# Overlapping feature tiles, B turned straight from DRAM, and the fourth state input of two chunks in one unit

## The chip, the core and the metric

The kernel runs on one core of a Trainium2 chip. The metric is the device time in microseconds. A core has five engines that run beside each other: TensorE (PE, matrix products into PSUM, which has eight banks), VectorE (DVE), ScalarE (ACT), GpSimd (POOL) and SyncE (SP, which issues the DMAs here). Each engine takes its instructions in the order in which they were written; semaphores tie the engines together.

## The reference

The input x has 2048 tokens of 448 features. It is normalised per token, and two branches read the result xn:

```python
xn = _layernorm(x)
# branch A: a diagonal complex recurrence over the tokens, 448 states
Lam_bar = exp(dt * (Lambda_re + 1j * Lambda_im));  B_bar = ((Lam_bar - 1) / Lam) * (B_re + 1j * B_im)
h_t = Lam_bar * h_{t-1} + B_bar @ xn_t
s = 2 * real(C @ h) + xn * Dskip
# branch B: a gated network with 1792 hidden features
g = silu((sigmoid(xn @ w_gate) * (xn @ w_up)) @ w_down)
out = x + s * g
```

## The kernel before

**Chunks and tiles.** The tokens go in four chunks of 512 (c = 0 to 3), each of four tiles of 128. The 448 features are the contracted dimension of most products. They are kept, turned, in `xnT[c]` as four tiles of 128 rows: features 0 to 127, 128 to 255, 256 to 383, and a fourth tile that holds features 384 to 447 twice, once in each half of 64 rows. The second copy is made by `ln_turn` (L272, chunk 0) and `ln_twice` (L277, the others) before the turning; PE turns chunk 0 (L274), DMA transposes on SP turn the others (L270). The weights of gate and up have the first 384 rows in `wg` and `wu`, and the last 64 rows of both stand under each other in `wt`: gate in the upper half of the rows, up in the lower half. So gate takes its tail from one copy of the features and up from the other.

**Halves.** From the fifth group of hidden features on, PE works with two halves of 64 rows that run beside each other. A sum (`Sum`, L504) has seven products of 64 rows, because 448 is seven times 64; some of them run in the upper half and some in the lower one. Where a sum changes halves, its next product waits for the last one of the other half by way of an empty instruction (a "word") in POOL's queue (L512). A unit is either one group of 128 hidden features (`gu_unit`, two sums, gate and up) or one state input (`bu_unit`). States 0 to 383 are three state inputs of two sums, real and imaginary. The fourth state input holds the last 64 states, real in one half of the output's partitions and imaginary in the other; it is one sum with four products in the upper half and three in the lower.

**Pairs of units.** `duo` (L1050) runs two units: first the upper half of the first unit beside the lower half of the second, then the other way round. Behind the second step ScalarE empties the four PSUM banks (the `empty` functions: sigmoid and a copy for a group of hidden features, L740; copies for a state input, L570 and L631), and what else stands in `beside` for that place is emitted (`rest`). `fill` then emits VectorE's pieces of the recurrence (phase factors, the scan along the tokens, phase factors again) as far as PE's time of that step allows; it takes them from the two oldest units that have any left. A line of each chunk gives the order of pairs (L1080 to L1083): negative numbers are state inputs, -4 being the fourth. `emit_downs` (the product with w_down of the chunk before) and `emit_ys` (the product with C) stand between them. In the fourth state input the halves of the partitions have to be swapped before VectorE can combine real and imaginary; two DMAs do this (`swap_halves`, L529), for the input and again after the scan.

**B and C.** B's real and imaginary rows are loaded into `raw_re` and `raw_im` as they are, the last 64 columns are doubled (L153, L288, L289), and eight DMA transposes (`emit_b`, L297) make `bT`, the stationary operand of the state inputs. C's rows are loaded in the second half of chunk 0 into `raw_c` and `raw_re` and turned by eight DMA transposes (L169) at the first two groups of chunk 1: first the four of `tc_re`, then the four of `tc_im`. `emit_c` (L457) mixes them into `ct`; each of its seven mixes is a scaled copy on ScalarE into a scratch (L482) and a product and sum on VectorE (L483). The first three ScalarE parts stand at `"down1"` of chunk 1, ahead of the reading of that chunk's down sums (sigd L764, zb L766). A list `c_room` (L467) says where the scratches lie: the first two in the room of `raw_im`, two in the pool's own, two in the room of `raw_c`, one in the pool's own. A room is written again only when all that read its earlier contents has ended.

**Order.** `keep_order` fixes the written order on each engine. SP's queue has, in order: x of chunk 0, the weights' columns 0 to 511, B, the weights' columns 512 to 1023, x of chunk 1, then the first B transpose, the weights' columns 1024 to 1791 with another B transpose between them, skip, four B transposes, x of chunk 2, two transposes of chunk 1's xn, the last two B transposes, two more of xn, w_down, C, and then the swaps and the C transposes.

Of the kernel before, what the change touches and what calls it, by code (L numbers as in the profile page):

```python
# [10 lines left out]
FP32 = mybir.dt.float32  # L11
# [18 lines left out]
NPK = 2 * D  # L30
EPS = 1e-5
# [7 lines left out]
def swap_pair(ap: bass.AP) -> bass.AP:  # L39
    step_p, n_p = ap.ap[0]  # L40
    step_m, n_m = ap.ap[1]
    step_f, n_f = ap.ap[2]
    assert n_m == 2
    return bass.AP(tensor=ap.tensor, offset=ap.offset + step_m,
                   ap=[[step_p, n_p], [-step_m, n_m], [step_f, n_f]])

# [17 lines left out]
def kernel(  # L64
# [51 lines left out]
    def load_rows(eng, t, mat, f0, f1):  # L116
        eng.dma_start(out=t[:, 0:3, f0:f1], in_=mat[0:384, f0:f1].rearrange("(kt p) f -> p kt f", p=P))
        eng.dma_start(out=t[0:64, 3, f0:f1], in_=mat[384:448, f0:f1])

    def load_w(eng, f0, f1, between=None):  # L120
        for t, mat in ((wg, B_w_gate), (wu, B_w_up)):
            eng.dma_start(out=t[:, :, f0:f1], in_=mat[0:384, f0:f1].rearrange("(kt p) f -> p kt f", p=P))
        if between:
            between()
        for mat, p0 in ((B_w_gate, 0), (B_w_up, 64)):
            eng.dma_start(out=wt[p0:p0 + 64, f0:f1], in_=mat[384:448, f0:f1])
# [130 lines left out]
    def ln_norm(c, j):  # L257
        t = c * TPC + j
        xb = xn[c % 3]
        if c < 2:  # L260
            dve.tensor_scalar(out=xb[:, j, 0:D], in0=x_t[c][:, j, :], scalar1=mv[:, t, 0:1],
                              scalar2=rsd[:, t, :], op0=ALU.subtract, op1=ALU.mult)
        else:
            act.activation(xb[:, j, 0:D], x_t[c][:, j, :], ACT.Identity, bias=nmr[:, t, :],
                           scale=rsd[:, t, :])

    def ln_turn(c, j):
# [4 lines left out]
        (dve if j < 2 else pool).tensor_copy(out=xb[:, j, D:DP], in_=xb[:, j, 384:D])  # L272
# [3 lines left out]
    def ln_twice(c, copy, j0=0, j1=TPC):  # L276
        copy(out=xn[c % 3][:, j0:j1, D:DP], in_=xn[c % 3][:, j0:j1, 384:D])  # L277
        for j in range(j0, j1):
            ln_turn(c, j)
# [6 lines left out]
    def emit_b_twice():  # L286
        t = raw["b_im"]
        act.copy(out=t[:, 0:3, D:DP], in_=t[:, 0:3, 384:D])  # L288
        act.copy(out=t[0:64, 3, D:DP], in_=t[0:64, 3, 384:D])  # L289

    def emit_b(cc, pt):
        n = P if pt < 3 else 64
        if cc == 0:
            p0 = pt * P
        else:
            p0 = D if pt == 3 else 512 + pt * P
        sync.dma_start_transpose(out=bT[:, :, p0:p0 + n], in_=raw[("b_re", "b_im")[cc]][0:n, pt, :])  # L297

    def bu_cols(pt, cc):
        if pt == 3:  # L300
            return 384, 512
        return (pt * P, (pt + 1) * P) if cc == 0 else (512 + pt * P, 512 + (pt + 1) * P)
# [104 lines left out]
    def emit_skip(c):  # L407

        t = xn[c % 3][:, :, 0:D]
        dve.tensor_tensor(out=t, in0=t, in1=bcast_mid(skip[:], TPC), op=ALU.mult)  # L410
# [46 lines left out]
    def emit_c(i):  # L457
# [9 lines left out]
        if not c_room:  # L467
            for nm in ("raw_im", "raw_c"):
                both = []
                c_room.extend((nm, both, k) for k in range(2))  # L470
                if nm == "raw_im":
# [57 lines left out]
    def swap_halves(o, i):  # L529
        sync.dma_start(out=o[0:64, :], in_=i[64:128, :])  # L530
        sync.dma_start(out=o[64:128, :], in_=i[0:64, :])

    def bu_unit(c, pt):
        u = Unit()
        psts = [bank("bu") for _ in range(2 if pt < 3 else 1)]
        sums = [Sum(t, 7) for t in psts]

        def ops(h, cc, n):
            lo, hi = bu_cols(pt, cc)
            return [(sums[cc], (bT[HALF[h], kt, lo:hi], xnT[c][HALF[h], kt, :], 0, TC))  # L540
                    for kt in range(n)]

        if pt < 3:
            u.top = ops(0, 0, 4) + ops(0, 1, 3)
            u.bot = ops(1, 0, 3) + ops(1, 1, 4)
        else:
            u.top, u.bot = ops(0, 0, 4), ops(1, 0, 3)
        u.empty, u.then = bu_after(c, pt, psts)
        return u

    def bu_after(c, pt, pst):
# [5 lines left out]

        def then():
            unread[0] += 1
            assert unread[0] <= 4  # L560
            stream[0] += 1
            popped[stream[0]] = clock[0]
            pieces.extend((*p, stream[0]) for p in line)
# [62 lines left out]
        else:  # L626
            bus = sp.tile([P, TC], BF16, name="bus3", tag="bus", bufs=4)
            bsw = sp.tile([P, TC], BF16, name="bsw3", bufs=1)

            def empty_3():  # L630
                act.copy(out=bus[:], in_=pst[0][:])  # L631
                swap_halves(bsw, bus)

            empty = [empty_3]

            def q0():
                T["ta"] = sp.tile([P, TC], BF16, name="ta3", tag="ta")
                dve.tensor_tensor(out=T["ta"][:], in0=bus[:], in1=cosT[:, 3, :], op=mul)
# [511 lines left out]
```

## Time and profile before

| what | value |
|---|---|
| runs of the kernel, device time | 184.78, 184.30, 184.43 us; median 184.43 |
| profiled execution, its span from first to last instruction | 182.6 us |
| PE busy | 177.7 us, 1644 products |
| VectorE busy | 165.0 us |
| ScalarE busy | 114.1 us |
| POOL busy | 24.5 us |
| DMA queue of SP, share of the 16 engines' span | 35.1%, 14.79 MB |
| granted TensorE clock | 1.000 |

The profile gives the span of its own execution and no other time for it; the runs' median lies 1.83 us above that span, for what lies before the first and after the last instruction. A line of the timeline has the start in us, the duration in us, the engine, the line of the program, the operation, what it writes and reads, and in brackets the idle time of the engine before it with what ended that. "SPq" is SP's queue: the duration there is that of issuing the DMA, not of the transfer. Products are pipelined: a product of 512 columns is shown with 0.38 us while another one starts every 0.216 us in the same half.

### The profile page before, as it was taken

What the parts mean: (1) busy time and instruction counts of PE and PEld (TensorE: products, weight loads), DVE (VectorE), ACT (ScalarE), POOL (GpSimd) and SP (SyncE); (2) the same over time, 40 slices, a digit from 0 to 9 for tenths busy, and PEclk for the clock granted to TensorE, in tenths of its full rate; (3) what the DMA queues carried; (4) which work ended last, traced back from release to release, by engine and by line L of the source; (5) the groups of instructions that cost most, each with busy time, mean ns of one, the idle gap of its engine ahead of it and who ended that gap; (6) DMA issues with size and microseconds to landing.
All of it is one profiled execution on the core that took longest, in us unless ns stands there. A gap on an engine that the chain in (4) does not pass through costs nothing.

```text
span 182.6 us, 4348 instructions
## 1 busy us (share of the span) xinstructions
PE 177.7 (97%) x1644; PEld 98.3 (54%) x1644; DVE 165.0 (90%) x337; ACT 114.1 (63%) x236; POOL 24.5 (13%) x61
## 2 busy tenths in 40 slices
PE   7999999999999999999999999999999999999992
PEld 7776644446654444645654445545665544645552
DVE  4899999799989979999999999599999999699983
ACT  3999577979487787997367766057048567144100
POOL 4768546321000000004000000000000000000000
PEclk9999999999999999999999999999999999999999
DMA  5999997895434113011251010030001000011112
GB/s 152 312 307 252 231 161 106 229 311 111 104 76 89 29 32 101 4 52 52 41 79 29 4 29 0 4 101 0 4 2 29 4 13 17 4 50 50 29 36 68
DMA packets 27659, 15.07 MB, mean 83 GB/s; under 512 B 16243, under 2 KB 27638, under 8 KB 27638
## 3 DMA queue, kind: packets, MB, share of 16 engines
q1 hardware_dynamic: 27632, 14.79, 35.1%
q8 instruction: 13, 0.21, 0.5%
q14 instruction: 8, 0.07, 0.2%
q10 hardware_dynamic: 6, 0.00, 0.0%
HBM read 8.49 MB, written 1.84 MB: 57 GB/s over the span
## 4 chain that ended last, share of the span: by engine, by line
PE 97%; DVE 1%; POOL 0%; issue 0%; POOLq 0%; DVEq 0%
PE g_ps L510 25%; PE u_ps L510 19%; PE d_ps L510 17%; PE bu L510 12%; PE y_ps L510 11%; PE d_ps L1093 6%; PE warm_ps L192 2%; PE g_ps L702 2%; PE u_ps L702 1%; PE tp_x L274 1%; PE g_ps L695 1%; DVE sg L846 0%; DVE o_l L852 0%; DVE xnT L282 0%; POOL ident L129 0%
## 5 line engine op out<-in xcount | busy, mean ns | idle before, releaser
L510 PE MATMUL u_ps<-xnT,wu 64*128 64x512 bf16 x312 | 68.9, 376 | 0.0
L510 PE MATMUL g_ps<-xnT,wg 64*128 64x512 bf16 x312 | 62.0, 376 | 0.0
L740 ACT ACTIVATE sig<-g_ps 128x512 bf16<-128x512 f32 x52 | 29.1, 597 | 29.1 <-PE g_ps L510 29.1
L510 PE MATMUL bu<-xnT,bT 64*128 64x512 bf16 x196 | 45.7, 376 | 0.0
L510 PEld LDWEIGHTS <-wu 64*128 64x128 bf16 x312 | 25.3, 94 | 17.8 <-POOLq L512 1.6
L510 PE MATMUL d_ps<-wd,hF 64*128 64x448 bf16 x336 | 32.9, 349 | 0.0
L510 PEld LDWEIGHTS <-wg 64*128 64x128 bf16 x312 | 22.7, 94 | 17.6 <-POOLq L512 1.9
L740 ACT CAST ub<-u_ps 128x512 bf16<-128x512 f32 x52 | 29.3, 604 | 0.8 <-DVE hF L712 0.8
L510 PEld LDWEIGHTS <-hF 64*128 64x128 bf16 x336 | 19.9, 94 | 12.1
L510 PEld LDWEIGHTS <-bT 64*128 64x128 bf16 x196 | 17.7, 94 | 10.7
L510 PE MATMUL y_ps<-ct,h 64*128 64x448 bf16 (+2 forms) x203 | 22.7, 343 | 0.0
L589 DVE TENSOR_TENSOR_SCAN wv<-r_col,st,ta 128x512 bf16<-128x512 f32 x18 | 22.6, 1274 | 0.1
L737 DVE TENSOR_TENSOR hF<-sig,ub 128x512 bf16<-128x512 bf16 x52 | 20.9, 416 | 1.3 <-ACT ub L740 1.1
L510 PE MATMUL u_ps<-xnT,wt 64*128 64x512 bf16 x52 | 19.6, 376 | 0.0
L510 PE MATMUL g_ps<-xnT,wt 64*128 64x512 bf16 x52 | 19.6, 376 | 0.0
L510 PEld LDWEIGHTS <-h 64*128 64x128 bf16 (+1 forms) x203 | 13.4, 95 | 8.0
L570 ACT CAST bus<-bu 128x512 bf16<-128x512 f32 x24 | 14.3, 595 | 2.3 <-PE g_ps L510 2.3
L764 ACT ACTIVATE sigd<-d_ps 128x448 bf16<-128x448 f32 x12 | 6.6, 550 | 12.4 <-PE d_ps L510 12.4
L238 POOL TENSOR_TENSOR rsd<-ve,mhalf 128x1 f32<-128x1 f32 (+2 forms) x8 | 7.5, 932 | 48.5 <-PE u_ps L510 45.6
L510 PEld LDWEIGHTS <-wt 64*128 64x128 bf16 x104 | 9.8, 94 | 5.5 <-DMA wt<-in_B_w_up_dram 0.4
L1093 PE MATMUL d_ps<-wd,hF 128*128 128x448 bf16 x56 | 10.9, 353 | 0.0
L819 DVE TENSOR_TENSOR o_t<-y_ps,xn 128x448 bf16<-128x448 f32 x12 | 6.9, 618 | 3.7 <-PE y_ps L510 3.7
(153 smaller groups left out, 229.8 us busy)
## 6 DMA issues: line engine op xcount, KB each, us to landing
wd<-in_B_w_down_dram SPq DMA_DIRECT2D x1, 1568.0 KB, 7.6
x<-in_A_x_dram SPq DMA_DIRECT2D x3, 448.0 KB, 5.5
out_dram<-o_t SPq DMA_DIRECT2D x6, 224.0 KB, 2.1
wg<-in_B_w_gate_dram SPq DMA_DIRECT2D x2, 384.0 KB, 4.4
wu<-in_B_w_up_dram SPq DMA_DIRECT2D x2, 384.0 KB, 5.3
wg<-in_B_w_gate_dram SPq DMA_DIRECT2D x1, 576.0 KB
wu<-in_B_w_up_dram SPq DMA_DIRECT2D x1, 576.0 KB, 8.6
bsw<-bus SPq DMA_DIRECT2D x8, 64.0 KB, 2.0
```

The source lines that it names most:

```text
L192: pe.matmul(warm_ps[:], lhsT=ident[:], rhs=ident[:], start=True, stop=True)
L238: pool.tensor_tensor(out=rsd[:, t:t + n, :], in0=ve[:, t:t + n, :], in1=mhalf[:, 0:n, :], op=ALU.pow)
L274: pe.transpose(tps[j % 2][:, kt, :], xb[:, j, kt * P:(kt + 1) * P], ident[:])
L510: m = pe.matmul(self.t[:, n0:n1], lhsT=lhsT, rhs=rhs, start=self.done == 1, stop=self.done == self.n)
L570: empty = [lambda cc=cc: act.copy(out=bus[:, cc, :], in_=pst[cc][:]) for cc in range(2)]
L589: dve.tensor_tensor_scan(out=T["wv"][:, cc, :], data0=rb, data1=T["ta"][:, cc, :], initial=(0.0 if c == 0 else st[pt][:, cc, :]), op0=mul, ...
L702: pe.matmul(t[:, n0:n1], lhsT=wm[:, kt, f0:f1], rhs=xnT[c][:, kt, n0:n1], start=(first and kt == 0), stop=(not first and kt == 2))
L737: dve.tensor_tensor(out=h[:], in0=sig[:], in1=ub[:], op=ALU.mult)
L740: u.empty = [lambda: act.activation(sig[:], gt[:], ACT.Sigmoid), lambda: act.copy(out=ub[:], in_=ut[:])]
L764: act.activation(sigd[:], ds[j][:], ACT.Sigmoid)
L819: dve.tensor_tensor(out=o[:, i, :], in0=ys[c, j + 2 * i][:], in1=xb[:, i, :], op=ALU.add)
L1093: pe.matmul(ds[j][:], lhsT=hF[c, ft][:, j * P:(j + 1) * P], rhs=wd[:, ft, :], start=ft == 0, stop=ft == FT - 1)
```

## The change

Seven things change together.

1. The four turned feature tiles begin at features 0, 128, 192 and 320 (`K_ROWS`), so that they overlap: tile 1 holds 128 to 255, tile 2 holds 192 to 319. Gate takes tiles 0, 2 and 3 whole and features 128 to 191 from the upper half of tile 1; up takes tiles 0, 1 and 3 whole and features 256 to 319 from the lower half of tile 2. The doubling copies (L272, L277) are no longer there. For chunks 1 to 3 the norm writes 512 columns, as two runs of 256 that overlap in the source; what reads xn later (skip, the last sums) reads two runs of 224.
2. B isn't loaded into SBUF. Four DMA transposes read it in DRAM, each 448 rows and 256 columns. The copies that doubled its last columns are gone. The columns of the fourth state input are gathered into `b3` by two POOL copies at group 9 of chunk 0.
3. `load_w` has six DMAs for a range of columns, not four, since the rows of gate and up are cut differently; the second range is 512 to 1279 and the third 1280 to 1791.
4. The fourth state input of chunks 0 and 1 is one unit with two sums, at its place in chunk 0, and that of chunks 2 and 3 one unit at its place in chunk 2. It has two banks, two ScalarE copies, one swap of twice the size, and one list of VectorE's pieces for both chunks.
5. In chunks 1 and 3 there is then no fourth state input; `duo` becomes `group`, which also takes three units, and (5,6), (-4,7) becomes (5,6,7) there.
6. With `raw_im` gone, the first two scratches of the mixing lie in the room of `raw_re`, and the scratches of the last chunk's rest in `raw_re` and `raw_c`.
7. The B transposes stand together on SP ahead of the weights' last columns.

```diff
+K_ROWS = (0, 128, 192, 320)
+GATE_K, UP_K = (0, 2, 3), (0, 1, 3)
...
+        eng.dma_start(out=wg[:, 1:3, f0:f1], in_=rows(B_w_gate, 192, 448))
+        eng.dma_start(out=wg[:, 0, f0:f1], in_=rows(B_w_gate, 0, 128))
+        eng.dma_start(out=wu[:, 0:2, f0:f1], in_=rows(B_w_up, 0, 256))
+        eng.dma_start(out=wu[:, 2, f0:f1], in_=rows(B_w_up, 320, 448))
+        eng.dma_start(out=wt[0:64, f0:f1], in_=rows(B_w_gate, 128, 192))
+        eng.dma_start(out=wt[64:128, f0:f1], in_=rows(B_w_up, 256, 320))
...
-    for nm, mat in (("b_re", A_B_re), ("b_im", A_B_im)):
-        raw[nm] = w.tile([P, KT, DP], BF16, name=nm, tag="raw" + nm[1:])
-        load_rows(sync, raw[nm], mat, 0, D)
-    dve.memset(raw["b_re"][:, :, D:DP], 0.0)
-    load_w(sync, 512, 1024)
+    load_w(sync, 512, 1280)
     load_x(1)
...
-        (dve if j < 2 else pool).tensor_copy(out=xb[:, j, D:DP], in_=xb[:, j, 384:D])
         for kt in range(KT):
-            pe.transpose(tps[j % 2][:, kt, :], xb[:, j, kt * P:(kt + 1) * P], ident[:])
+            pe.transpose(tps[j % 2][:, kt, :], xb[:, j, K_ROWS[kt]:K_ROWS[kt] + P], ident[:])
...
+    def emit_b(cc, kt):
+        sync.dma_start_transpose(out=bT[:, kt:kt + 2, cc * D:(cc + 1) * D],
+                                 in_=(A_B_re, A_B_im)[cc][:, K_ROWS[kt]:K_ROWS[kt] + 2 * P])
+
+    b3 = w.tile([P, KT, P], BF16, name="b3")
+
+    def emit_b3():
+        for cc in range(2):
+            pool.tensor_copy(out=b3[:, :, cc * 64:(cc + 1) * 64], in_=bT[:, :, cc * D + 384:(cc + 1) * D])
...
-            for nm in ("raw_im", "raw_c"):
+            for nm in ("raw_re", "raw_c"):
...
+    def bu_pair_after(c, psts):
+        bus = sp.tile([P, 2, TC], BF16, name="bus3", tag="bus", bufs=4)
+        bsw = sp.tile([P, 2, TC], BF16, name="bsw3", bufs=1)
+        a, b = [bu_after(c + i, 3, (bus[:, i, :], bsw[:, i, :])) for i in range(2)]
+
+        def empty(i):
+            act.copy(out=bus[:, i, :], in_=psts[i][:])
+            if i == 1:
+                swap_halves(bsw, bus)
...
-    emit_b(0, 0)
-    load_w(sync, 1024, F, lambda: emit_b(1, 0))
+    for cc in range(2):
+        for kt in (0, 2):
+            emit_b(cc, kt)
+    load_w(sync, 1280, F)
     sync.dma_start(out=skip[:], in_=A_Dskip.partition_broadcast(P))
-    for pt in range(1, KT - 1):
-        for cc in range(2):
-            emit_b(cc, pt)
...
-    at(0, 7, 0.0, lambda: [emit_b(cc, KT - 1) for cc in range(2)])
+    at(0, 9, 0.0, emit_b3)
...
+    def group(c, units):
+        top = sum((u.top for u in units), [])
+        bot = sum((u.bot for u in units[1:] + units[:1]), [])
+        t0, last = 0, len(units) - 1
+        for k, u in enumerate(units):
+            t1 = t0 + len(u.top)
             beside_each(top[t0:t1], bot[t0:t1])
+            whole = [units[0]] * (k == last) + [u] * (k > 0)
+            for i in range(2):
+                for v in whole:
+                    v.empty[i]()
...
-        emit_line(c, ((0, -1), (1, -2), emit_downs, (2, 3), (4, -3), (5, 6), (-4, 7), (8, 9), (10, 11), *ends))
+        mid = ((5, 6), (-4, 7)) if c == 2 else ((5, 6, 7),)
+        emit_line(c, ((0, -1), (1, -2), emit_downs, (2, 3), (4, -3), *mid, (8, 9), (10, 11), *ends))
```

More of the change, by code (lines that the diff above doesn't have):

```diff
@@ L529, in swap_halves, with ops @@
     def swap_halves(o, i):
-        sync.dma_start(out=o[0:64, :], in_=i[64:128, :])
-        sync.dma_start(out=o[64:128, :], in_=i[0:64, :])
+        sync.dma_start(out=o[0:64], in_=i[64:128])
+        sync.dma_start(out=o[64:128], in_=i[0:64])
     def bu_unit(c, pt):
         u = Unit()
-        psts = [bank("bu") for _ in range(2 if pt < 3 else 1)]
+        psts = [bank("bu") for _ in range(2)]
         sums = [Sum(t, 7) for t in psts]
[L538 to L541, printed above, removed]
+        def ops(h, i, n):
+            x = xnT[c + i * (pt == 3)]
+            return [(sums[i], (b_cols(HALF[h], kt, pt, i), x[HALF[h], kt, :], 0, TC))
+                    for kt in (range(KT) if n == KT else (UP_K, GATE_K)[h])]
@@ L551, in bu_after, with queue @@
+    def queue(line):
+        unread[0] += 1
+        assert unread[0] <= 4
+        stream[0] += 1
+        popped[stream[0]] = clock[0]
+        pieces.extend((*p, stream[0]) for p in line)
     def bu_after(c, pt, pst):
@@ L556, in later @@
             line.append((cost, fn, wait))
[L558 to L563, printed above, removed]
         rb = K["r"][:, pt:pt + 1].to_broadcast((P, TC))
@@ L670, in q7 @@
             def q7():
-                h = ht.tile([P, TC], BF16, name="h3")
+                h = ht.tile([P, TC], BF16, name="h3", bufs=3)
                 dve.tensor_tensor(out=h[:], in0=T["tcs"][:], in1=T["td"][:], op=add)
                 hs[c, 3] = h
-            for cost, f, wait in ((0.42, q0, 1), (0.42, q1, 2), (0.42, q2, 0), (1.27, q3, 0), (0.42, q4, 0),
-                                  (0.42, q5, 3), (0.34, q6, 0), (0.42, q7, 0)):
-                later(cost, f, wait)
-        return empty, then
+            return q0, q1, q2, q3, q4, q5, q6, q7
+        return empty, lambda: queue(line)
     hF = {}
@@ L911, in ln_plan @@
             at(own, "down0", 0.0, lambda j=j: ln_norm(c, j))
-        at(own, "down0", 0.0, lambda: ln_twice(c, act.copy))
+        at(own, "down0", 0.0, lambda: [ln_turn(c, j) for j in range(TPC)])
     dummy = w.tile([P, 1], FP32, name="dummy")
```

137 lines of the change are left out of this document (58 added, 79 removed).

## The prediction

> **What bounds the kernel now.** I read the page's totals and its chain first. All times below are on the profile's clock.
>
> ```profile
> span 182.6 us, 4348 instructions
> ...
> PE 177.7 (97%) x1644; PEld 98.3 (54%) x1644; DVE 165.0 (90%) x337; ACT 114.1 (63%) x236; POOL 24.5 (13%) x61
> ...
> PE 97%; DVE 1%; POOL 0%; issue 0%; POOLq 0%; DVEq 0%
> ```
>
> The chain that ended last is TensorE from end to end, so time is won by PE columns or PE stalls removed and lost where PE is made to wait. VectorE at 90% only matters if PE comes to wait for it: in the waits it idles for the finished sums of y in three chunks (3.7 us), so it catches up once a chunk. Next the timeline of PE, group by group. Two halves of 64 rows run beside each other; a full pair of units starts a pair of products each 0.216 us and takes 3.02 us for 14 of them. The groups with the fourth state input are the exception:
>
> ```profile
> 61.30 0.38 PE L510 MATMUL bu<-xnT,bT 64*128 64x512 bf16 x1
> 61.30 0.38 PE L510 MATMUL u_ps<-xnT,wu 64*128 64x512 bf16 x1
> 61.52 0.38 PE L510 MATMUL bu<-xnT,bT 64*128 64x512 bf16 x1
> 61.79 0.39 PE L510 MATMUL g_ps<-xnT,wg 64*128 64x512 bf16 x1
> 61.80 0.39 PE L510 MATMUL u_ps<-xnT,wu 64*128 64x512 bf16 x1
> ```
>
> One product runs alone at 61.52, the next starts 0.27 after it, and the same small hole comes at 62.73: the sum that changes halves waits for the word through POOL, too soon after its last product. This group runs from 60.66 to 63.17, 2.51 us for 11 places of 0.216 (2.37).
>
> Then the queues that the change reorders. ScalarE in the second chunk's downs:
>
> ```profile
> 45.23 0.40 ACT L277 COPY xn<-xn 128x256 bf16<-128x256 bf16 x1
> 48.22 1.23 ACT L482 ACTIVATE c_tmps<-tc_re,nci 128x448 f32<-128x448 bf16 x2 [2.58 <-DMA tc_re<-c_re]
> 49.35 0.65 ACT L482 ACTIVATE c_tmp<-tc_re,nci 128x448 f32<-128x448 bf16 x1
> 49.91 0.52 ACT L764 ACTIVATE sigd<-d_ps 128x448 bf16<-128x448 f32 x1
> ...
> 53.30 0.55 ACT L766 CAST zb<-d_ps 128x448 bf16<-128x448 f32 x1
> ```
>
> ScalarE stands 2.58 us for C's turned halves and is free just as the first d sums are done. SP's queue of the same stretch:
>
> ```profile
> 31.66 0.57 SPq L1025 DMA_DIRECT2D wd<-in_B_w_down_dram  x1
> ...
> 37.49 1.11 SPq L530 DMA_DIRECT2D bsw<-bus  x1
> 38.65 0.60 SPq L531 DMA_DIRECT2D bsw<-bus  x1
> 41.16 5.78 SPq L169 DMA_TRANSPOSE tc_re<-c_re  x4
> 47.04 5.86 SPq L169 DMA_TRANSPOSE tc_im<-c_im  x4
> ```
>
> The real turns end first, the imaginary ones 5.9 us later (landed 54.1, where VectorE's mixing idles 0.8). And POOL, whose queue also carries the words between halves:
>
> ```profile
> 25.44 0.20 POOL L380 TENSOR_TENSOR a_re<-r_col,cs 128x4 f32<-128x4 f32 x1 [1.58 <-PE u_ps L510]
> 25.73 0.55 POOL L381 TENSOR_SCALAR a_re<-a_re 128x4 f32<-128x4 f32 x1
> 26.25 0.72 POOL L382 TENSOR_TENSOR a_im<-r_col,sn 128x4 f32<-128x4 f32 x1
> ```
>
> **The change part by part.**
>
> *Start, -0.45.* The copies of the last 64 features go: 0.18 and 0.21 on VectorE, 0.23 and 0.24 on POOL.
>
> ```profile
> 5.72 0.21 DVE L272 COPY xn<-xn 128x64 bf16<-128x64 bf16 x1
> ```
>
> The second tile's fourth turn waits for the copy that ends at 5.93; without it the turns follow the norm's end at 5.68, and with two of VectorE's places free both copies out of PSUM end 0.14 earlier, so PE's first product at 6.79 moves by 0.14. At the fourth tile the norm ends at 9.11, POOL's copy at 9.40, and PE stands until about 9.7 (chain: 0.53 for four turns that took 0.24 before). That is another 0.3. Gate weights come now in two DMAs and 0.4-0.6 more issue each; the same bytes land at 5.9 and are wanted at 6.6. Bounds: 0.14 to 0.55.
>
> *Middle, -0.99.* (5,6) with (-4,7) took 3.02+2.51=5.53; three feature groups take 21 places, 4.53: -1.00, in chunks two and four. (-4,13) and (-4,7) of chunks one and three grow from 2.51 to 3.02: +0.51 each. Sum -1.00x2+0.51x2=-0.98 to -0.99. No place runs single any more and the holes go, because each sum now changes halves four places after its last product. What is late next: after three groups six of eight banks are held. ScalarE reads a bank every 0.47 us; group six is read two thirds into the last place, 1 us before (8,9) needs its banks, group five only 0.5 to 1.3 after. The trace doesn't say which bank is handed on. The first freed is the natural one: 0; if it is group five's, 0.55 in chunk four and 1.3 in chunk two, where three mixing operations of 0.65 stand on ScalarE.
>
> *Weights, -0.11.* Group (-1,8) takes 3.13: it waits for columns 1024 on, which now come with the earlier load. B's plain loads (0.8 MB) leave the queue, the larger load adds 0.46 MB, so what is wanted at 14.2 (landed 13.6 now) lands about 1 us earlier.
>
> *B's turns, 0.* Eight turns out of SBUF (1.2 to 2.2 us of SP each) become four out of DRAM of 448x256. No row has one. The bounds: 1.2 us, a turn's price whatever its rows (64 or 128 cost alike), and 3.5 x 1.27=4.4 if it goes by rows. By elements it is 1.75 x 1.27=2.2, and I take that, since the packets are the same 256 bytes: issues from 9.86 to 18.7, landed by 20.2. The second sum of (-1,8) wants them at 20.6 to 21.1. Behind them on SP stand the six remaining weight loads (0.57 each, to 22.2, wanted at 26), skip, x of chunk three and the turns of chunk two (norms ready at 22.7 to 23.7 anyway). Two B turns (3.0 us of SP) between the turns and wd are gone, so wd goes at about 28.4 against 31.66.
>
> *b3, +0.2.* Two POOL copies of 128x256 join the queue at 25.4 ahead of a_re. The 128x255 rows cost 0.41 to 0.65, so 1.0 together; with the 1.53 of the three rows above POOL is free at 28.0, and the second half of (-3,10) wants its word by 27.8. Both ends move alike. 0.2; bounds 0 and, with copies as slow as the 128x510 rows (up to 1.07), 1.3. [...]
>
> *C's scratch, +0.5.* This is the cost that the diff hides. The first two mixing scratches move from the room of b_im to that of raw_re, which now holds C's imaginary rows until their four turns have landed. So ScalarE's first c_tmps waits for the imaginary turns, not the real ones, and sigd and zb, which empty PE's d banks, queue behind it. From c_tmps to the end of the last zb it is 1.69 plus seven steps of 0.43 plus 0.55: 5.3 us. PE's (4,-3) wants the last of those banks at about 55.4 (start 54.6 less 0.05, fifth product), so the turns may land until 50.1 at no cost, and each us after that is a us of PE. When do they land? SP is freed earlier by 3 us, but the bsw swap stands before the turns and waits for the second bus copy of the new pair, about 36.8 (bus now 35.78, 0.56 earlier, two more ScalarE steps and one duration). Swap 1.1 to 1.7, eight turns 10.3 (at 1.29) to 11.7 (as the rows stand, with two longer issues of 1.9 and 2.0), landing 1.2: 49.4 to 51.6. I take 50.6, between them, since the long issues come about one in seven on SP: 0.5; bounds 0 and 1.5, or 4.0 if nothing on SP comes earlier (54.1). VectorE's four gates wait with the zb; its idle there is as PE's.
>
> *The rest, 0.* Norms write 512 for 448 (about 0.05 each on VectorE and ScalarE) and lose copies of 0.19 x2 and 0.40 x2. Skip and the last sums read two runs for one; same elements, off the path. The fourth input of chunks two and four is done a chunk early: 4.1 us of VectorE move from the tail (166.8 to 172.8 in this trace) into chunk three, where it idles 1.6 at y; y of the tail starts right behind, with h now that of the third input at the same place, so the end follows PE.
>
> Sum: -0.45-0.99-0.11+0.2+0.5=-0.85. The span of 182.6 becomes 181.75. The runs' median of 184.43 is 1.83 above the span, and I keep that: 183.6.
>
> **The rivals.** (a) *No new wait bites*: the turns land before 50.1 and POOL is in time, -1.55: 182.9. For it: SP freed by 3 us. Against: the swap. (b) *The scratch wait takes the gain*: turns as the rows stand, 51.6, cost 1.5: 184.4. (c) *It takes more than the gain*, the other side: SP isn't freed, because the DRAM turns or wd's landing hold it, and the imaginary turns land at 54.1 as now. ScalarE then holds PE 4.0; net +2.45: 186.9. It decides from 51.65 on (50.1+1.55). (d) *The turns out of DRAM cost by rows*, 4.4 each: landed at 29, so (-1,8) stands 8 us: 191. Against: 64 rows cost as much as 128. (e) *Group five's banks are handed on*: +1.85 on my sum: 185.4. (f) *POOL's copies run slowly beside VectorE*, at the 1.07 us of the slowest 128x510 row instead of 0.5: the word of (-3,10) comes 1.1 later still, 0.2 becomes 1.3: 184.7. [...]
>
> **How the numbers follow.** Mine 0.37, (a) 0.15, (b) 0.17, (c) 0.12, (d) 0.05, (e) 0.07, (f) 0.07. About 0.3% (0.55 us) is what a measurement tells from no change: faster is below 183.88, slower above 184.98. Mine is faster in most of its spread (0.33 of 0.37), (a) wholly, (b) in 0.03: 0.51. Within: 0.04 of mine, 0.12 of (b), 0.05 of (f): 0.21. Slower: (c), (d), (e), the rest of (b) and (f): 0.28. The range from 182.8 to 186.1 leaves out (d), most of (c) and a little below (a), together 0.2. My case alone is 183.1 to 184.0.
>
> **What would show it.** PE's first product near 6.65 and the step at 9.7 near 9.25; (-4,x) and (5,6,7) at 3.02 and 4.53; ScalarE's idle before c_tmps now ending on tc_im's landing, and whether (4,-3) of the second chunk is longer than 3.02; (-3,10) longer than 3.02 by POOL; the DRAM turns' issue time; (8,9) after three groups. It is wrong if the imaginary turns land far from 50.6, or if PE comes to wait for VectorE, which I price at nothing.

## The result and the profile after

The changed kernel takes 186.3 us (median of 186.16, 186.64, 186.00 and 186.43) against 184.37 of the kernel before (four runs, one more than in the table ahead): ratio 1.0107, 95% interval 1.0088 to 1.0127. It is slower by 1.1%, and the prediction of 183.6 us (182.8 to 186.1) had the wrong sign; the time lies 0.2 above its range. The page of the changed kernel:

```profile
span 184.1 us, 4339 instructions
...
PE 177.6 (96%) x1644; PEld 114.0 (62%) x1644; DVE 164.0 (89%) x332; ACT 113.3 (62%) x232; POOL 27.3 (15%) x61
...
PE 79%; ACT 6%; SPq 6%; POOL 2%; DMA 2%; issue 2%; DVE 1%; POOLq 0%; ACTq 0%; DVEq 0%
```

TensorE's work is the same, but the chain that ended last is no longer TensorE from end to end: a fifth of it runs over ScalarE, SP's queue, POOL and a landing. TensorE's timeline, read group by group (from the first product of a group to the first of the next), says where. All times are on the profile's clock.

| group | before | after | difference |
|---|---|---|---|
| start of (4,5) | 14.19 | 14.06 | -0.13 |
| (4,5) | 3.03 | 3.17 | +0.14 |
| (-1,8) | 3.13 | 3.02 | -0.11 |
| (-2,9) | 3.02 | 4.26 | +1.24 |
| (-4,13); (-4,7) of the third chunk | 2.51; 2.52 | 3.02; 3.02 | +1.01 |
| (5,6) and (-4,7), now (5,6,7), chunks two and four | 5.54; 5.52 | 4.53; 4.53 | -2.00 |
| (4,-3) of the second chunk | 3.02 | 4.76 | +1.74 |
| the y sums and (12,13) of the last chunk | 8.62 | 8.43 | -0.19 |

The differences add up to 1.70, and TensorE begins the last chunk's product with w_down 1.69 later (163.00 and 164.69). The last output ends 0.1 to 0.2 nearer to it, hence 1.5 to 1.6 us of span.

The intended part is there. TensorE's timeline in the fourth input's group of the third chunk shows a pair of products each 0.216 us and no hole, where the group of before had one product alone and then 0.27 us:

```profile
106.27 0.38 PE L509 MATMUL bu<-xnT,b 64*128 64x512 bf16 x1
106.29 0.38 PE L509 MATMUL u_ps<-xnT,wu 64*128 64x512 bf16 x1
106.48 0.38 PE L509 MATMUL bu<-xnT,b 64*128 64x512 bf16 x1
106.50 0.38 PE L509 MATMUL u_ps<-xnT,wu 64*128 64x512 bf16 x1
```

Two waits cost more than that won. The first is in (-2,9). TensorE stands before the second half of the group, released by POOL's queue, which carries the words:

```profile
24.67 0.38 PE L509 MATMUL u_ps<-xnT,wt 64*128 64x512 bf16 x1
26.02 0.39 PE L509 MATMUL g_ps<-xnT,wg 64*128 64x512 bf16 x1 [0.98 <-POOLq L511]
```

POOL's own timeline there, in the changed kernel; the instructions are those of the denominator (`emit_den`) and the first of the two b3 copies:

```profile
22.49 0.19 POOL L363 TENSOR_TENSOR t<-vec 128x4 f32<-128x4 f32 x1
22.64 0.36 POOL L364 TENSOR_TENSOR t<-vec 128x4 f32<-128x4 f32 x1
23.09 0.25 POOL L365 TENSOR_TENSOR den<-t,t 128x4 f32<-128x4 f32 x1
23.42 2.49 POOL L366 TENSOR_SCALAR t<-den 128x4 f32<-128x4 f32 x1
...
26.53 0.59 POOL L297 COPY b<-bT 128x256 bf16<-128x256 bf16 x1
```

An instruction over four columns takes 2.49 us. The same one before the change:

```profile
23.34 0.24 POOL L368 TENSOR_SCALAR t<-den 128x4 f32<-128x4 f32 x1
```

VectorE beside it, in the changed kernel:

```profile
22.22 1.38 DVE L268 TENSOR_SCALAR xn<-x,mv,rsd 128x512 bf16<-128x512 bf16 x4
23.52 1.09 DVE L745 TENSOR_TENSOR hF<-sig,ub 128x512 bf16<-128x512 bf16 x3
24.52 0.68 DVE L593 TENSOR_TENSOR ta<-bus,cosT 128x1024 bf16<-128x1024 bf16 x1
25.12 0.68 DVE L597 TENSOR_TENSOR tb<-bus,spm 128x1024 bf16<-128x1024 bf16 x1
25.84 0.69 DVE L600 TENSOR_TENSOR ta<-ta,tb 128x1024 bf16<-128x1024 bf16 x1
```

Three hF, ta and tb, each with two tensor inputs, follow each other without a gap from 23.52 to 25.80; then 35 ns pass before the next ta, which waits for tb. POOL's instruction begins 0.1 ahead of that run and ends 0.1 behind it.

The second is in (4,-3) of the second chunk. ScalarE's timeline:

```profile
53.58 1.23 ACT L481 ACTIVATE c_tmps<-tc_re,nci 128x448 f32<-128x448 bf16 x2 [6.64 <-DMA tc_im<-c_im]
54.71 0.65 ACT L481 ACTIVATE c_tmp<-tc_re,nci 128x448 f32<-128x448 bf16 x1
55.27 0.52 ACT L772 ACTIVATE sigd<-d_ps 128x448 bf16<-128x448 f32 x1
...
58.24 0.58 ACT L774 CAST zb<-d_ps 128x448 bf16<-128x448 f32 x1
```

It idles 6.64 us, and what ends it is the imaginary turns' landing, not the real ones' as before. TensorE waits for the zb behind it, one bank after the other:

```profile
56.27 0.38 PE L509 MATMUL g_ps<-xnT,wg 64*128 64x512 bf16 x1
57.13 0.37 PE L509 MATMUL bu<-xnT,bT 64*128 64x512 bf16 x1 [0.49 <-ACT zb L774]
...
58.00 0.37 PE L509 MATMUL bu<-xnT,bT 64*128 64x512 bf16 x1
58.87 0.37 PE L509 MATMUL u_ps<-xnT,wu 64*128 64x512 bf16 x1 [0.50 <-ACT zb L774]
```

### The profile page after: what moved, and what is told of

Its sections match the earlier page's. It is cut to its first block, busy times and chain, and to the rows that moved or that the text cites. A ratio compares the mean times of both kernels' runs of the same rounds, so it can differ in the third digit from the quotient of the medians.

```text
span 184.1 us, 4339 instructions
## 1 busy us (share of the span) xinstructions
PE 177.6 (96%) x1644; PEld 114.0 (62%) x1644; DVE 164.0 (89%) x332; ACT 113.3 (62%) x232; POOL 27.3 (15%) x61
## 4 chain that ended last, share of the span: by engine, by line
PE 79%; ACT 6%; SPq 6%; POOL 2%; DMA 2%; issue 2%; DVE 1%; POOLq 0%; ACTq 0%; DVEq 0%
PE g_ps L509 20%; PE u_ps L509 16%; PE d_ps L509 12%; PE y_ps L509 11%; PE bu L509 8%; PE d_ps L1103 6%; SPq L172 5%; PE warm_ps L195 2%; DMA tc_im<-c_im 2%; PE g_ps L709 2%; PE u_ps L709 1%; POOL t L366 1%; ACT sig L748 1%; ACT sigd L772 1%; ACT ub L748 1%
## 5 line engine op out<-in xcount | busy, mean ns | idle before, releaser
L509 PE MATMUL u_ps<-xnT,wu 64*128 64x512 bf16 x312 | 60.3, 376 | 0.5 <-ACT zb L774 0.5
L509 PE MATMUL g_ps<-xnT,wg 64*128 64x512 bf16 x312 | 54.8, 376 | 1.0 <-POOLq L511 1.0
L509 PE MATMUL bu<-xnT,bT 64*128 64x512 bf16 x168 | 37.7, 376 | 0.5 <-ACT zb L774 0.5
L509 PEld LDWEIGHTS <-wu 64*128 64x128 bf16 x312 | 24.7, 94 | 13.3 <-issue 0.3
L509 PE MATMUL d_ps<-wd,hF 64*128 64x448 bf16 x336 | 32.4, 349 | 0.0
L509 PEld LDWEIGHTS <-wg 64*128 64x128 bf16 x312 | 22.0, 94 | 15.1 <-POOLq L511 1.9
L509 PEld LDWEIGHTS <-hF 64*128 64x128 bf16 x336 | 23.2, 94 | 8.8
L509 PE MATMUL y_ps<-ct,h 64*128 64x448 bf16 (+2 forms) x203 | 22.2, 343 | 0.0
L509 PEld LDWEIGHTS <-bT 64*128 64x128 bf16 x168 | 15.6, 94 | 7.1 <-issue 0.8
L509 PEld LDWEIGHTS <-h 64*128 64x128 bf16 (+1 forms) x203 | 12.9, 95 | 8.6
```

The source lines that it names most:

```text
L509: m = pe.matmul(self.t[:, n0:n1], lhsT=lhsT, rhs=rhs, start=self.done == 1, stop=self.done == self.n)
```

## The experiments

Two theories were to be told apart from their rivals: that each of the two waits is one cause with one price (the room of the scratches; VectorE's run of two-input instructions), and that the pairing alone carries the gain. Spans are those of the profiled executions; the span before is 182.6, after 184.1.

| kernel | median us | ratio to before, 95% interval | span |
|---|---|---|---|
| e1_room | 184.92 | 1.0039 (1.0025 to 1.0052) | 183.2 |
| e2_den | 185.06 | 1.0046 (1.0032 to 1.0060) | 183.1 |
| e3_gaps | 185.49 | 1.0062 (1.0049 to 1.0076) | 183.7 |
| e7_longer_norms | 185.31 | 1.0041 (1.0019 to 1.0062) | 183.2 |
| e5_room_den | 183.31 | 0.9950 (0.9933 to 0.9968) | 180.9 |
| e4_pair | 183.36 | 0.9954 (0.9942 to 0.9967) | 181.7 |
| e9_overlap | 184.36 | 1.0014 (1.0003 to 1.0025) | 182.4 |
| e10_copies | 183.19 | 0.9951 (0.9939 to 0.9963) | 181.3 |
| e6_mirror | 183.45 | 0.9949 (0.9931 to 0.9967) | 182.0 |
| e8_b3_dma | 183.81 | 0.9971 (0.9957 to 0.9986) | 181.9 |
| e11_mirror_late | 183.38 | 0.9956 (0.9944 to 0.9968) | 181.1 |
| e12_both_moved | 183.07 | 0.9931 (0.9913 to 0.9949) | 181.1 |

**The scratches in the other room.** In the changed kernel:

```diff
-            for nm in ("raw_re", "raw_c"):
+            for nm in ("raw_c", "raw_re"):
...
-                if nm == "raw_re":
+                if nm == "raw_c":
```

> One part of the changed kernel is undone in effect: the first two scratches of the mixing lie in the room of C's real rows, which is free when the real turns have landed, and the third pair lies in the room of C's imaginary rows. Theory: in the changed kernel (4,-3) of the second chunk took 4.76 us instead of 3.02 because ScalarE's first scratch waits for the imaginary turns (6.6 us idle, ended by the landing at 53.5). Then ScalarE waits for the real turns only, as before the change, (4,-3) is 3.02 again, and the span falls by 1.74 to about 182.4; (-2,9) stays at 4.26. Rival: PE's stall there has another cause (the later downs, VectorE's mixing, the turns of C later as a whole), and the scratch's wait is only the last of several: then (4,-3) stays above 3.5 us and the span falls by less than 1.0.

(4,-3) is 3.02. ScalarE's timeline of this kernel:

```profile
47.63 1.23 ACT L481 ACTIVATE c_tmps<-tc_re,nci 128x448 f32<-128x448 bf16 x2
...
51.63 0.54 ACT L772 ACTIVATE sigd<-d_ps 128x448 bf16<-128x448 f32 x1 [2.21 <-PE d_ps L509]
```

The first scratch starts 5.95 earlier, behind the norms and with no wait, and sigd waits for TensorE again and not the other way. The whole 1.74 is thus the room: the imaginary turns landed at 54.4 in this execution, 0.9 later than in the changed kernel and half a us after (2,3) had begun, and cost nothing. In (-2,9) POOL's instruction took 2.49 us again. The span fell by 0.9 only, since this execution lost elsewhere: (6,7) began 0.26 later, and (-3,10) took 3.49 for 3.02, its words behind b3 copies that took 1.80 us here and 0.94 in the changed kernel.

**The denominator early.** In the changed kernel:

```diff
     emit_steps()
+    emit_den()
...
-    for ft, cost, fn in ((6, 0.0, emit_constants), (8, 0.0, emit_den), (9, 0.1, emit_inv), (9, 0.0, emit_a),
+    for ft, cost, fn in ((6, 0.0, emit_constants), (9, 0.1, emit_inv), (9, 0.0, emit_a),
```

> One part of the changed kernel is moved: the six POOL instructions of the denominator (t, t, den, t, den and their neighbours) stand early in POOL's queue, ahead of the sines, and not at group 8 of the first chunk. Theory: in the changed kernel the fourth of them took 2.49 us for 0.24, and the words of (-2,9)'s second half stood behind it. With it away, (-2,9) is 3.02 for 4.26 and the span falls by about 1.24 to 182.9; (4,-3) of the second chunk keeps its 4.76, since its wait moves with what stands ahead of it. Rival: the next instruction of POOL in that stretch (the b3 copies) is held up in its place, and (-2,9) or (-3,10) is still long: then the span stays within 0.4 of 184.1.

(-2,9) is 3.02, (4,-3) 4.76, the span 183.1. As the theory has it, with a little of the rival: POOL's next work in that stretch, the copies of B's columns, took 1.58 us, and (11,12), whose words stand behind it and a_re, took 3.15.

**Gaps put back into VectorE's run.** In the changed kernel, behind each two norms of the second chunk:

```diff
+        tail = xn[1][:, j0:j0 + 2, D:DP]
+        dve.tensor_copy(out=tail, in_=tail)
```

> Work is added to the changed kernel and nothing is taken from it: behind each two norms of the second chunk VectorE copies the last 64 columns of two tiles onto themselves, twice in all, about 0.19 us each, as the copies that the change removed did; each has to wait for the norm ahead of it. Theory: POOL's 128x4 instruction took 2.49 us because VectorE ran without a gap from 22.2 to 25.8; the copies put gaps of some 35 ns back, POOL's instruction takes 0.3 to 0.8 us again, (-2,9) is 3.02, and the span falls by about 1.2 to 182.9, although VectorE does 0.4 us more. Rival: the instruction was slow by itself or for something else than VectorE (its code being loaded, the DMAs of that moment): it keeps 2.5 us, (-2,9) keeps 4.26, and the span is 184.1 or a little more.

With 0.4 us more work on VectorE, POOL's instruction takes a tenth of the time, and (-2,9) is 3.02:

```profile
23.24 0.24 POOL L366 TENSOR_SCALAR t<-den 128x4 f32<-128x4 f32 x1
```

So it was VectorE's order beside it, and the instruction is not slow by itself. The span is 183.7, not 182.9: C's turns landed later against TensorE in this execution, and the scratch's wait took 2.48 (the section on why the prediction was wrong works this out). Why the copies helped was still open, because they do two things: they put gaps in, and they start the run of two-input instructions 0.3 later, at 23.83.

**A later run without gaps.** In the changed kernel, at the same place:

```diff
+        t, src = TPC + j0, two_runs(x_t[1][:, j0, :], 192, 2 * P)
+        dve.tensor_scalar(out=xn[2][:, j0, :], in0=src, scalar1=mv[:, t, 0:1], scalar2=rsd[:, t, :],
+                          op0=ALU.subtract, op1=ALU.mult)
```

> Work is added to the changed kernel and nothing is taken from it: behind each two norms of the second chunk VectorE does one more norm (0.33 us, one tensor input) into a tile that nobody reads. It waits for nothing ahead of it, so it puts no gap into VectorE's run; it only makes the run of instructions with two tensor inputs (three hF, ta, tb) start 0.65 later. Theory: the gaps are not what counts. POOL's small instructions took 0.19 to 0.36 us beside the norms even without gaps, and the fourth took 2.49 us because the run with two inputs began before it had read; before the change that run began 0.37 later, when the denominator was done. Then the fourth takes 0.24 us here, (-2,9) is 3.02 and the span about 182.9. Rival: what counts is the gap of 35 ns: without one the instruction takes 2.5 to 3.2 us, (-2,9) is 4.3 to 4.9, and the span is 184.1 to 184.8.

VectorE of this kernel has six norms and then the run, with no gap until 26.3:

```profile
23.04 0.73 DVE L268 TENSOR_SCALAR xn<-x,mv,rsd 128x512 bf16<-128x512 bf16 x2
23.69 0.41 DVE L1028 TENSOR_SCALAR xn<-x,mv,rsd 128x512 bf16<-128x512 bf16 x1
24.01 1.09 DVE L745 TENSOR_TENSOR hF<-sig,ub 128x512 bf16<-128x512 bf16 x3
25.02 0.69 DVE L593 TENSOR_TENSOR ta<-bus,cosT 128x1024 bf16<-128x1024 bf16 x1
```

and POOL:

```profile
23.27 0.28 POOL L366 TENSOR_SCALAR t<-den 128x4 f32<-128x4 f32 x1
23.64 0.20 POOL L367 TENSOR_TENSOR den<-den,t 128x4 f32<-128x4 f32 x1
25.14 2.23 POOL L297 COPY b<-bT 128x256 bf16<-128x256 bf16 x2 [1.30 <-PE u_ps L509]
```

The denominator is done before 24.01, and (-2,9) is 3.02. The gaps were not what mattered: a norm has one tensor input, and POOL's small instructions ran beside it at 0.19 to 0.37 us. The run with two inputs is what had held POOL for 2.49 us, and the change had moved it forward by 0.37 us, onto the denominator. Before the change it began here, 0.3 behind the end of POOL's instruction at 23.34:

```profile
23.89 1.09 DVE L737 TENSOR_TENSOR hF<-sig,ub 128x512 bf16<-128x512 bf16 x3
```

Moved back by 0.5 in e7_longer_norms, it catches the b3 copies (2.23 us for two), and (-3,10) and (11,12) pay with 3.18 and 3.64.

**Both waits gone.** The edits of e1_room and e2_den together.

> Both suspected waits are taken from the changed kernel at once: the first two scratches in the room of C's real rows, and the denominator early in POOL's queue. Theory: the two waits are separate costs, 1.74 and 1.24 us, and they are all that the change lost. Then (-2,9) and (4,-3) are both 3.02, the span is 181.1 to 181.3, the median about 183.2, and the kernel is faster than before the change (ratio 0.994). Rival: the waits share a cause or cover a third one (POOL's b3 copies beside VectorE, x of chunk three, the turns of chunk two): the span stays at 182 or more and the ratio is not below 0.997.

(-2,9) and (4,-3) are both 3.02, and the chain is TensorE's again:

```profile
PE 96%; DVE 1%; issue 0%; POOL 0%; POOLq 0%; DVEq 0%
```

Median 183.31, ratio 0.995. The two waits are separate, and without them the change is a gain of 0.5%. The span of 180.9 lies under the expectation because TensorE started 0.37 earlier in this execution (last section).

**The pairing alone.** On the kernel before, with `bu_unit`, `bu_pair_after` and `group` of the changed one:

```diff
-            for nm in ("raw_im", "raw_c"):
+            for nm in ("raw_c", "raw_re"):
...
-        emit_line(c, ((0, -1), (1, -2), emit_downs, (2, 3), (4, -3), (5, 6), (-4, 7), (8, 9), (10, 11), *ends))
+        mid = ((5, 6), (-4, 7)) if c == 2 else ((5, 6, 7),)
+        emit_line(c, ((0, -1), (1, -2), emit_downs, (2, 3), (4, -3), *mid, (8, 9), (10, 11), *ends))
```

> The pairing alone, on the kernel before the change: the fourth state input of two chunks in one unit and three feature groups at once in chunks two and four. B is loaded and turned as before, the features don't overlap, the copies stay. (For room, B's imaginary rows share a room with C's real rows, the first two scratches lie there too, and the rests in raw_re and raw_c.) Theory: the pairing is worth its columns, -1.00 twice and +0.51 twice, and brings no wait of its own: span 181.6 for 182.6, median about 183.4 for 184.4, ratio 0.9946. Rival: the larger unit brings waits that the other parts of the change had covered or shared (banks after three groups, the one swap of twice the size, VectorE behind in chunk three): the span is 182.2 or more.

All groups of the middle are as in the changed kernel and none is longer: span 181.7, ratio 0.9954. The pairing alone is worth what the whole change is worth once its two waits are gone.

**The overlap alone.** The kernel with both waits gone, with `bu_unit` and `duo` of before:

```diff
-        mid = ((5, 6), (-4, 7)) if c == 2 else ((5, 6, 7),)
-        emit_line(c, ((0, -1), (1, -2), emit_downs, (2, 3), (4, -3), *mid, (8, 9), (10, 11), *ends))
+        emit_line(c, ((0, -1), (1, -2), emit_downs, (2, 3), (4, -3), (5, 6), (-4, 7), (8, 9), (10, 11), *ends))
```

> The other half alone: overlapping feature tiles, B from DRAM and the new cut of the weights, without the pairing (units and groups as before the change), with both waits taken away (scratches in the room of C's real rows, denominator early). Theory: the pairing is worth all of the gain (0.98), and this half is worth nothing or little: the copies at the start lay beside TensorE's own slow turns, what is won at the fourth tile is lost again at (4,5) behind POOL's mirror copies, and only the 0.11 of (-1,8) is left. Span 182.3 to 182.6, ratio 0.998 to 1.000. Rival, as predicted before: the start is worth 0.45 and the weights 0.11, ratio 0.997 or below.

Ratio 1.0014: nothing won, perhaps 0.1% lost. Its groups say why: (-1,8) and (-4,13) are 0.11 shorter each, (4,5) is 0.15 and (11,12) 0.13 longer, both for words behind POOL's copies, as the runs further down show.

**The first copies put back**, in the kernel with both waits gone:

```diff
+        (dve if j < 2 else pool).tensor_copy(out=xb[:, j, 384:D], in_=xb[:, j, 384:D])
         for kt in range(KT):
             pe.transpose(tps[j % 2][:, kt, :], xb[:, j, K_ROWS[kt]:K_ROWS[kt] + P], ident[:])
```

> The kernel with both waits gone, with copies at the start put back: ahead of each tile's turns in the first chunk the last 64 columns are copied onto themselves, on VectorE for two tiles and on POOL for two, as the kernel before did with its second copies. Theory: they were hidden, or what they cost is taken up again at (4,5), so the ratio stays at 0.995 and the time within 0.15 of the kernel without them (183.3). Rival, as predicted before: they cost 0.45, and the ratio goes to 0.9975 (183.75).

183.19 against 183.31, ratios 0.9951 and 0.9950: the copies cost nothing that these runs can tell.

**POOL's other work ahead of words.** First the mirrors of two of the four state inputs, from the start to behind (4,5)'s words:

```diff
-    for pt in (0, 1, 3, 2):
+    for pt in (0, 1):
...
+    at(0, 5, 0.0, lambda: [emit_mirror(pt) for pt in (3, 2)])
```

> As the kernel with both waits gone, and two of the four mirror copies of cosine and sine on POOL (states 384 to 447 and 256 to 383) stand behind the words of (4,5) and not ahead of them. Theory: the gain at the start (PE's first group of halves starts 0.13 earlier) is lost because the words of (4,5)'s second half stand behind POOL's mirror copies, so (4,5) takes 3.17 to 3.36 us in the changed kernel and (6,7) starts at the same time in all. With the copies behind the words (4,5) is 3.02 to 3.04 and the span is 0.13 to 0.2 shorter than without this edit. Rival: the second half of (4,5) waits for something else (ScalarE's or VectorE's work on the first groups, the weights): (4,5) stays at 3.17 or more and nothing is won; or the copies, run later beside VectorE, hold up the words of (6,7) instead.

(4,5) falls to 3.03, but (6,7) rises to 3.65. The rival's last clause was right, and nothing was won. That (4,5) had lost the start's gain to POOL's mirror copies is not shown by this run alone, since the group began at 14.39 here, and in three kernels that began it near 14.2 with the mirrors ahead (before, e4_pair, e10_copies) it is 3.03 too; in e1_room, which began it at 14.24, it is 3.25. With B's columns gathered by DMA besides:

```diff
-            pool.tensor_copy(out=b3[:, :, cc * 64:(cc + 1) * 64], in_=bT[:, :, cc * D + 384:(cc + 1) * D])
+            sync.dma_start(out=b3[:, :, cc * 64:(cc + 1) * 64], in_=bT[:, :, cc * D + 384:(cc + 1) * D])
...
     load_x(2)
+    emit_b3()
...
-    at(0, 9, 0.0, emit_b3)
```

> As the kernel with both waits gone and the mirrors moved; besides, the fourth input's columns of B are gathered by two DMAs behind x of chunk three on SP's queue, not by two POOL copies. Theory: POOL's copies took 1.6 us beside VectorE where the denominator stood early, and made (11,12) 3.15 for 3.02; without them (11,12) is 3.02 and the span is another 0.1 shorter, the two DMAs (0.6 us each on SP) cost nothing, because chunk one's norms come 1 us after them at the earliest. Rival: SP is then late for the turns of chunk one's norms, w_down or C, and nothing is won or 0.2 to 1.2 is lost at the first pairs of chunk one.

(11,12) is 3.02, so POOL's copies are what it had waited for, and the two DMAs hold up nothing. (6,7) is still 3.63. The ratio of 0.9971 is no better than that of e6_mirror, although no group is longer; in the profiled execution the stretch from the last chunk's product with w_down to the end took 19.72 us and 19.44 there, which no run explains. Then the mirrors behind the words of (6,7), with B's columns on POOL again:

```diff
-    at(0, 5, 0.0, lambda: [emit_mirror(pt) for pt in (3, 2)])
+    at(0, 7, 0.0, lambda: [emit_mirror(pt) for pt in (3, 2)])
     at(0, 7, 1.0, lambda: second_chunk(0))
```

> As the kernel with both waits gone, and POOL's mirror copies for the last two state inputs stand behind the words of (6,7), not of (4,5). Theory: placed at (4,5) they took 0.15 from that group and put 0.6 on (6,7), because a mirror copy that runs while words are due holds them whatever the group; behind (6,7) POOL has about 3 us before the words of (-1,8), so (4,5) and (6,7) are both 3.02 to 3.04 and the span is 0.15 to 0.3 shorter than with the mirrors ahead of all (median about 183.1). Rival: the copies now run beside VectorE's two-input instructions or push back the power of chunk one's variances, which stands behind them, and (-1,8) or chunk one's first pairs become longer: nothing won, or a loss of 0.3 or more.

(4,5) is 3.03 and (6,7) 3.02. Here (4,5) began at 13.70, as in the kernel with both waits gone, where it took 3.17: so it was the mirrors. Now (11,12) takes 3.35, behind b3 copies of 1.78 us, and the ratio is 0.9956. Each copy that was moved gave its time back a group or several later. Last, both edits together, the DMAs for B's columns and the mirrors behind (6,7):

> The kernel with both waits gone, the two late mirrors behind the words of (6,7), and the fourth input's columns gathered by two DMAs on SP and not by POOL. Theory: what is left of the loss is whatever stands on POOL ahead of words that are due: 0.15 at (4,5) with the mirrors ahead of it, 0.13 to 0.35 at (11,12) with the copies of B's columns, each of which came back elsewhere when only one was moved. With both gone all groups of the first chunk are 3.02 to 3.04, and the kernel is at 183.0 to 183.2 (ratio 0.994), 0.15 to 0.3 below the kernel with the mirrors moved alone. Rival: a third wait appears, on POOL (the powers of the variances) or on SP (the two DMAs ahead of chunk one's turns), and the ratio is 0.995 to 0.997.

All groups of the first chunk are 3.02 or 3.03. POOL's lines of this kernel, mirrors in a stretch where no word is due:

```profile
18.89 0.40 POOL L449 COPY cosT<-cosT 128x255 bf16<-128x255 bf16 x1 [2.01 <-PE u_ps L509]
19.23 0.62 POOL L451 COPY spm<-spm 128x510 bf16<-128x510 bf16 x1
```

183.07 us, ratio 0.9931: the lowest of all, though its interval overlaps those of e5_room_den and e4_pair.

## Why the prediction was wrong

Two steps carry the miss, with 1.24 us each. The step on POOL followed what the change adds to POOL's queue, and put what the removed copies do to VectorE's order beside it at nothing; and the step on C's scratch had the right wait, but took too little for the time from the last issue to the landing. The gain at the start, 0.46 more, was not there. Step by step:

*Middle, -0.99:* right. -2.00 and +1.01 in the profile, and -0.9 of span for the pairing alone. The rival that group five's banks are handed on didn't come: (8,9) is 3.02 behind the three groups.

*Weights, -0.11:* right, 3.13 to 3.02; in the pairing alone, which keeps the old loads, the group took 3.06, so part of it may be the execution. *B's turns, 0:* right; the four took 1.41, 3.48, 2.14 and 1.45 us of SP (8.5 together, for the estimated 8.8), and the last landed at 20.1, estimated 20.2. That the sum came out so close is in part luck: the step gave each turn 2.2 us.

*C's scratch, +0.5:* the mechanism was right and the size wrong, 1.74. The step's rule was right: by TensorE's timeline (2,3) of the second chunk began at 53.25, 52.20, 52.07 and 52.63 in the changed kernel, e2_den, e3_gaps and e7_longer_norms; ScalarE's first scratch began 0.33, 0.35, 1.07 and 0.00 later, and (2,3) and (4,-3) together were 1.74, 1.75, 2.48 and 1.40 too long. That is the delay plus 1.40 in all four, to within 0.01, one us for each us; the prediction's bound of 50.1 lay 1.43 ahead of its (2,3). Mis-sized was the landing. The changed kernel's imaginary turns landed at 53.5 and not 50.6. 1.6 of that is the swap, issued at 38.41 for 36.8 since TensorE was late by then; this nearly cancels, because (2,3) was late by 1.7 too. The rest is the time from the end of the last issue to the landing: 2.4 us, 2.8 in e2_den and about 3.1 in e7_longer_norms, where the prediction took the 1.2 of the one execution before. (Its upper end, 51.6, is 51.4 by the terms that it gives, and cases (b) and (c) leave out its own 0.2 for b3; neither makes up the difference.) The chain of waits of the changed kernel, in order of time, shows the last turn standing 3.67 us from its issue on:

```profile
48.53 1.26 SPq L172
49.80 0.04 issue
49.84 3.67 DMA tc_im<-c_im
```

*b3, +0.2, and rival (f):* here a step was missing. The prediction put VectorE's hold on POOL at the b3 copies, and followed what the change adds to POOL's queue. It did not follow what the removed copies do to VectorE's order beside the POOL work already there: +1.24 at the denominator. (-3,10), where the 0.2 was expected, is 3.02; with the denominator moved (e2_den) it is 3.02 too, and the copies cost 0.13 at (11,12). Beside VectorE's run of five instructions with two tensor inputs POOL's 128x4 instruction took 2.49 us, in the changed kernel and in e1_room, and was not let in between them; beside the norms, which have one, POOL's small instructions took 0.19 to 0.37 us. Whether it is the second input that makes the difference was not shown. In the prediction this was rival (f), with a chance of 0.07 and a price of 1.1 us, at another instruction.

*Start, -0.45:* failed, 0. It was in two parts. The first read the second tile's fourth turn as waiting for the copy that ends at 5.93. But that tile's turns start at 5.74, 5.83, 5.93 and 6.04 before the change and at 5.74, 5.82, 5.93 and 6.04 after it: the fourth stood behind the third, and the copy held up nothing. The first product did not move with the copies: 6.87 in the changed kernel and 6.88 in the pairing alone, which has the copies and the same slow turns. The fourth tile's step gained 0.13, and (4,5) lost it behind POOL's mirrors, a queue that the step had not followed to the next word: its second half begins at 15.71 in both kernels.

Together: Start +0.46, the denominator +1.24, the scratch +1.24, b3 -0.2 and the last pair of the last chunk -0.19, which no step named and no run explains, lead from the predicted -0.85 to the 1.70 of TensorE. That 186.3 lies near the 186.9 of rival (c) is chance: there SP isn't freed and the scratch alone costs 4.0, while here w_down was issued at 29.11 for 31.66 before, and the scratch cost 1.74.

## What to carry to other kernels

Work that is taken off an engine moves what stands behind it forward (here by 0.37 us); ask which instruction of another engine was lying just beside that work. Where a queue carries other engines' signals, a small instruction's price is what can hold it there (2.49 us here, for 0.24), and a copy moved within such a queue is only gone if no signal is due while it runs (the mirrors: (6,7) at 3.65 in e6_mirror, 3.02 in e11_mirror_late). When scratch space changes its room, the wait to price is that for the last reader of the room, up to the landing and not to the issue (2.4 us apart in the changed kernel); and a change of several parts should be priced so that each part has to earn its place: here one part had the whole gain.

## What was not expected of the hardware

**POOL held through several instructions.** A 128x4 instruction took 2.49 us, through three hF, ta and tb back to back, until a gap of 35 ns, in the changed kernel and again in e1_room. It is not so in every case: in the kernel before, a 128x4 product on POOL took 0.20 beside ta and tb (25.44), so when POOL gets in between two instructions was not settled. VectorE may be held too: in e3_gaps a b3 copy began inside ta, and the following tb took 0.88 us for 0.68; but in e7_longer_norms a copy began inside ta as well, and tb kept its 0.69 while the two copies took 2.23.

**The DMA turn ahead of a long issue lands late.** In the fourteen traces, from 38 us on, 41 of 224 DMA turns take 0.6 to 1.25 us longer to issue than the usual 1.2 to 1.3. In the changed kernel such an issue came right behind the last imaginary turn, whose landing is the 3.67 above:

```profile
51.20 1.85 SPq L279 DMA_TRANSPOSE xnT<-xn  x1
```

Of the turns of usual length whose landing the traces show, the 22 ahead of a long issue landed 3.67 to 4.42 us after their own start, and the 78 others 2.37 to 2.56. Which of the two brings the other about, and why, was not tried.

**The start differs from execution to execution.** TensorE's turns of a tile at the start follow each other after 0.107 us in some executions (a little less between the first two) and after 0.056 in others. The changed kernel:

```profile
5.10 0.61 PE L282 MATMUL tp_x<-ident,xn 128*128 128x128 bf16 x4
...
6.87 1.14 PE L709 MATMUL g_ps<-xnT,wg 128*128 128x256 bf16 x9
```

The kernel with both waits gone, whose start differs by the denominator on POOL alone (e3_gaps, whose start is the same to the instruction, has the fast turns too, and its first product at 6.65):

```profile
5.10 0.40 PE L282 MATMUL tp_x<-ident,xn 128*128 128x128 bf16 x4
...
6.62 1.14 PE L709 MATMUL g_ps<-xnT,wg 128*128 128x256 bf16 x9 [0.24 <-DVE xnT L285]
```

The change from one rate to the other fell ahead of the first turn (5.1 us of the span) in some executions and behind the eighth (6.0) in others. In the kernels without the copies whose first turn began by 5.15, the first product came at 6.62 to 6.88 and the first group of halves at 13.70 to 14.10; the page's row of the granted clock shows 9 there in all of them. What sets the moment was not shown; it differs between executions whose start is the same to the instruction (first product at 6.87 in the changed kernel, at 6.65 in e3_gaps). So a start's tenths can't be read from one execution of each kernel, which is how the prediction read them, and only the repeated runs of e10_copies weigh the copies.
